# Reading the bias band backwards, warming TensorE with dummy matmuls, reordering and merging weight loads, and moving three copies to ScalarE in an attention kernel with T5 bias and a following feed-forward layer

## The chip, the cores and the metric

One core of one Trainium2 chip. The metric is the device time of one execution in microseconds (us), from the median of several executions. The granted TensorE clock of an execution is the mean over its span (1.00 is full speed). Ratios are computed as the mean time of one kernel's fast runs over that of the other kernel's fast runs of the same rounds on the same chip, with a 95% interval; so a ratio is not quite the ratio of the medians that stand beside it.

Engines: PE is TensorE, DVE is VectorE, ACT is ScalarE, POOL is GpSimd, SP is SyncE.

## The reference

Attention with a T5 relative-position bias over B=8, H=8, S=576, D=64, then a feed-forward layer over 4608 tokens (512 to 2048 to 512). Cut to what matters:

```python
scores = scale * np.matmul(q, k.transpose(0, 1, 3, 2))
bucket = ...                      # from |i - j|; constant for |i - j| >= 128
bias = bias_table[bucket]
scores = scores + bias.transpose(2, 0, 1)[None, :, :, :]
attn = softmax(scores)            # cut
attn_out = np.matmul(attn, v)
x = attn_out.transpose(0, 2, 1, 3).reshape(B * S, H * D)
h = x @ w_in
g = np.maximum(0.01 * h, h)
out = g @ w_out
```

The bias depends on the distance alone, and it is one constant from distance 128 on. So the kernel multiplies exp(score) by exp(bias minus that constant) inside a band around the diagonal and by nothing outside.

## The kernel before

The kernel works on 32 *pairs* (two heads of one batch; four pairs per batch) in program order. For a pair: copy q and k into rows (`pr`, DVE), transpose them (PE) and copy the result out of PSUM (`qt`, `kt`), score matmuls (`ps_s`, PE), exponential (`at`, `at4`, ACT), multiply by the band (DVE), then in the next pair's turn multiply by v (`ps_o`, called AV here, PE), normalise (`opair`, DVE) and transpose into `xT`. From pair 4 on, pieces of the feed-forward layer are put between these on PE.

The band: a row `ub` of 512 numbers per head is made from the bias table, written to DRAM (`u_row`) and read back as `hk`, in which each partition holds the row shifted by one. In `hk` the columns run the wrong way, so POOL (pairs 1 to 3) and DVE (pair 0) copy it reversed into `eb`, and a piece of that into `eb4` for the last 64 keys.

```python
nc.sync.dma_start(out=udr.ap(), in_=ub)                      # u_row
for h0, h1 in ((0, 2), (2, H)):
    nc.sync.dma_start(out=hk[:, h0:h1, :], in_=...)          # shifted by one per partition

def make_band(eng, p):
    t = hk[:, 2 * p : 2 * p + 2, :]
    eng.tensor_copy(out=eb[:, 2 * p : 2 * p + 2, :],
                    in_=...)                                 # t with its last step -1
    for e in range(2):
        r = slice(e * SL, (e + 1) * SL)
        eng.tensor_copy(out=eb4[r, p, :], in_=eb[r, 2 * p + e, e * SL : e * SL + P + SL])

load_qk(0, 2, H)
for i in range(NBUF):
    ...                                   # DVE clears v4, vn, kt, at, at4 of both buffers
load_v(0, 0, 2, True)
load_v(0, 2, H, False)
for j in range(1, n_pairs):
    make_band(nc.gpsimd, j)               # POOL waits here for hk
# ... cut ...
for n in range(N + 1):
    if n == 0:
        load_qk(1, 0, H)                  # all of these are issued by POOL, in this order
        load_w_in(0)                      # 4 loads of 256 KB
        load_w_in(1)                      # 4 loads
        load_v(1, 0, H, False)            # v of batch 1: needed by the AV of pair 4
        load_w_out()                      # 4 loads
    # ... cut ...

def band(n, u):
    # ... cut ...
    elif u == NJ + 1:
        o, m = at4[:, 3 * P : S], eb4[:, p, :]
    nc.vector.tensor_tensor(out=o, in0=o, in1=m, op=ALU.mult)
```

The softmax here doesn't subtract the row's maximum and nothing guards it: scores larger than these inputs give would overflow.

## Time and profile before

Median 418.32 us (three runs, 418.28 to 418.84). The profile is of one more execution, of 419.69 us (its span, first to last instruction, is 417.9 us).

| stretch of the profile before | PE busy |
|---|---|
| 0 to 60 us | 42.5 of 60 |
| 60 to 100 us | 38.2 of 40 |
| 100 to 200 us | 100.0 of 100 |
| 200 to 300 us | 100.0 of 100 |

After 60 us PE has next to no gaps, so time can only come from the first 60. The way to read those is by the start of each pair (its first 64x512 score matmul, from the timeline): 10.0, 15.1, 24.4, 30.6, 37.2, 45.2, 57.0 us, then every 8.5. The successor's start minus its own is a pair's length: pair 1 takes 9.3 and pair 5 takes 11.8 us, where neighbours take 6.3 and 8.5.

Busy time in windows of the kernel before. The columns are the window; its length; then PE, PE's weight loads, DVE, ACT and POOL, each as busy us and (instructions); the granted clock; the DMA share; GB/s:

```profile
20.00:25.00 5.00, 4.20 (x52) 2.94 (x50) 4.47 (x12) 2.92 (x4) 4.67 (x9) 1.00 0.01 3
...
45.00:50.00 5.00, 2.84 (x35) 1.48 (x35) 1.61 (x4) 3.02 (x4) 2.19 (x4) 1.00 1.72 183
50.00:55.00 5.00, 5.00 (x62) 2.98 (x58) 2.57 (x7) 2.69 (x4) 4.06 (x6) 0.66 1.24 207
```

At 20 to 25 the DMA engines move 3 GB/s: nothing is asked of them. At 45 to 50 PE has only 2.84 us of work, and then the clock falls to 0.66, so the 5.00 busy us that follow are partly slow ones.

Why nothing is asked of DMA is seen in POOL's timeline (start, us, engine, line, operation, out<-in, count, and in brackets what ended the idle time before it):

```profile
18.11 1.07 POOL L177 COPY eb<-hk 128x768 bf16<-128x768 bf16 x1 [3.79 <-DMA hk<-u_row]
...
23.98 0.81 POOL L109 DMA_DIRECT2D qn_100<-in_q_dram  x1
24.78 0.77 POOL L109 DMA_DIRECT2D kn_102<-in_k_dram  x1
25.54 3.24 POOL L204 DMA_DIRECT2D w_in_sb<-in_moe_w_in_dram  x6
...
35.08 0.89 POOL L125 DMA_DIRECT2D vn_104<-in_v_dram  x1 [1.37 <-DVE opair L327]
37.44 2.88 POOL L125 DMA_DIRECT2D vn_104<-in_v_dram  x3 [1.47 <-DMA w_in_sb<-in_moe_w_in_dram]
```

POOL waits 3.79 us for `hk`, copies until 24, and only then asks for the next batch and the weights. `vn_104` is v of batch 1; it stands behind both halves of `w_in`, and its last parts are asked for at 37.4 and later. The waits of PE in the first 62 us (what waits <- what it waits for: us, times, longest) and PE's timeline show where that ends:

```profile
PE ps_tq L231 <- DVE pr L223: 7.8, 1, 7.8
...
PE ps_o L321 <- DMA vn_104<-in_v_dram: 2.2, 2, 1.4
```

```profile
48.24 0.19 PE L321 MATMUL ps_o<-vn_104,at_109 128*128 128x65 bf16 x1 [1.41 <-DMA vn_104<-in_v_dram]
49.17 0.19 PE L321 MATMUL ps_o<-vn_104,at_109 128*128 128x65 bf16 x1 [0.74 <-DMA vn_104<-in_v_dram]
...
51.45 0.63 PE L347 MATMUL pm_865<-xT_92,w_in_sb 128*128 128x512 bf16 x1
...
55.15 0.38 PE L347 MATMUL pm_925<-xT_92,w_in_sb 128*128 128x512 bf16 x1
```

AV of pair 4 waits 2.2 us for v, and the same matmul that takes 0.38 us at 55 takes 0.63 at 51. Before pair 2 the chain of waits runs through the band: the row's write to DRAM, then `hk` for all heads:

```profile
4.99 4.93 DMA u_row<-ub
...
10.38 7.68 DMA hk<-u_row
...
18.11 1.08 POOL eb L177
```

Last, the band multiplies by form (mean ns in the middle, after the busy us):

```profile
L308 DVE TENSOR_TENSOR at_109<-at_109,eb 128x768 bf16<-128x768 bf16 x32 | 17.6, 552 | 16.3 <-ACT at_109 L279 16.3
...
L308 DVE TENSOR_TENSOR at_109<-at_109,eb 128x512 bf16<-128x512 bf16 x16 | 6.8, 424 | 20.5 <-ACT at_109 L279 20.3
```

### The profile page before, as it was taken

How to read it: one execution, taken by the hardware profiler on the slowest of the kernel's cores; microseconds unless marked ns; L12 is line 12 of the kernel's file. 1: busy time of each engine (PE TensorE's matmuls, PEld its weight loads, DVE VectorE, ACT ScalarE, POOL GpSimd, SP SyncE). 2: the span in 40 equal slices, each digit the busy share in tenths (PEclk: the TensorE clock that was granted, in tenths of full speed). 3: DMA queues.
4: the chain of work that ended last, by engine and by line, in shares of the span. 5: the costliest groups of instructions: out<-in, count | busy, mean ns of one | idle time of the engine just before them, and what ended most of it. 6: DMA issues, size and time to landing. Idle time of an engine off the chain costs nothing.

```text
span 417.9 us, 9069 instructions
## 1 busy us (share of the span) xinstructions
PE 394.9 (94%) x3872; PEld 203.8 (49%) x3872; DVE 226.7 (54%) x585; ACT 247.0 (59%) x339; POOL 67.9 (16%) x97
## 2 busy tenths in 40 slices
PE   1897699999999999999999999999999999999996
PEld 1365365455555555445554455555555454444442
DVE  6789667765666655655566666655666431010111
ACT  1768477866666676666666666667666633333310
POOL 8474631301022100410041004000000000000000
PEclk9999999999999999999999999999999999999999
DMA  8969999458027710944091706300000001010112
GB/s 115 131 99 202 183 204 166 36 33 140 27 37 71 123 44 27 83 75 91 25 83 30 137 27 39 46 25 27 27 27 27 27 27 50 25 52 25 52 50 76
DMA packets 60096, 29.16 MB, mean 70 GB/s; under 512 B 39056, under 2 KB 54424, under 8 KB 60056
## 3 DMA queue, kind: packets, MB, share of 16 engines
q0 software_dynamic: 53536, 18.36, 40.5%
q1 hardware_dynamic: 6520, 10.24, 6.8%
q8 instruction: 30, 0.49, 0.5%
q14 instruction: 10, 0.08, 0.1%
HBM read 37.49 MB, written 9.45 MB: 112 GB/s over the span
## 4 chain that ended last, share of the span: by engine, by line
PE 82%; DMA 8%; ACT 3%; POOL 2%; DVE 2%; issue 1%; SPq 0%
PE ps_o L321 7%; PE ps_s L259 6%; DMA w_in_sb<-in_moe_w_in_dram 3%; DMA vn_104<-in_v_dram 2%; PE ps_s L268 2%; PE ps_o L323 2%; DMA hk<-u_row 2%; PE ps_tx L335 2%; PE ps_tq L231 1%; PE ps_tk L242 1%; PE ps_s L265 1%; ACT at_109 L279 1%; DMA u_row<-ub 1%; PE pm_5795 L358 1%; PE pm_4291 L358 1%; PE pm_4115 L358 1%
## 5 line engine op out<-in xcount | busy, mean ns | idle before, releaser
L347 PEld LDWEIGHTS <-w_in_sb 128*128 128x128 bf16 x576 | 50.0, 98 | 73.3 <-issue 22.6
L279 ACT ACTIVATE at_109<-ps_s 128x1024 bf16<-128x1024 f32 x64 | 64.4, 1021 | 22.7 <-PE ps_s L259 22.6
L358 PEld LDWEIGHTS <-gt 128*128 128x128 bf16 x576 | 52.5, 98 | 51.4 <-issue 0.4
L279 ACT ACTIVATE at_110<-ps_s 128x1024 bf16<-128x1024 f32 x64 | 64.8, 1021 | 20.1 <-PE ps_s L259 20.1
L308 DVE TENSOR_TENSOR at_110<-at_110,eb 128x512 bf16<-128x512 bf16 (+1 forms) x64 | 32.5, 510 | 44.4 <-ACT at_110 L279 39.7
L308 DVE TENSOR_TENSOR at_109<-at_109,eb 128x512 bf16<-128x512 bf16 (+1 forms) x64 | 32.0, 505 | 39.0 <-ACT at_109 L279 36.6
L321 PEld LDWEIGHTS <-at_109 128*128 128x128 bf16 x640 | 29.3, 101 | 13.2 <-DVE opair L327 3.9
L327 DVE TENSOR_TENSOR opair<-ps_o,rcp 128x320 bf16<-128x320 f32 x64 | 31.5, 491 | 2.2
L321 PEld LDWEIGHTS <-at_110 128*128 128x128 bf16 x640 | 27.8, 99 | 10.0 <-DVE opair L327 3.0
L125 POOL DMA_DIRECT2D vn_104<-in_v_dram x16 | 14.2, 898 | 70.0 <-PE ps_o L323 39.9
L234 DVE COPY qt<-ps_tq 128x576 bf16<-128x576 bf16 x32 | 23.9, 747 | 0.5 <-PE ps_tq L231 0.5
L259 PE MATMUL ps_s<-qt,kt_107 64*128 64x512 bf16 x128 | 21.4, 403 | 2.1 <-DVE kt_107 L245 1.2
L125 POOL DMA_DIRECT2D vn_103<-in_v_dram x16 | 13.9, 881 | 55.5 <-PE ps_o L323 53.0
L231 PE MATMUL ps_tq<-ident,pr 96*128 96x96 bf16 x192 | 14.2, 213 | 7.9 <-DVE pr L223 7.8
L259 PE MATMUL ps_s<-qt,kt_108 64*128 64x512 bf16 x128 | 20.9, 398 | 0.7 <-ACT at_110 L279 0.3
L326 DVE RECIPROCAL rcp<-ps_o 128x5 f32<-128x5 f32 x64 | 12.2, 190 | 14.6 <-PE ps_o L323 14.6
L321 PE MATMUL ps_o<-vn_103,at_109 128*128 128x65 bf16 x320 | 16.1, 200 | 2.4 <-DVE opair L327 2.1
L321 PE MATMUL ps_o<-vn_104,at_109 128*128 128x65 bf16 x320 | 15.4, 197 | 2.2 <-DMA vn_104<-in_v_dram 2.2
L323 PEld LDWEIGHTS <-at_0_111 128*128 128x128 bf16 x160 | 16.1, 100 | 1.1 <-issue 0.8
L321 PE MATMUL ps_o<-vn_103,at_110 128*128 128x65 bf16 x320 | 15.1, 197 | 1.5 <-DVE opair L327 1.5
L281 ACT ACTIVATE at_110<-ps_s 128x512 bf16<-128x512 f32 x16 | 9.6, 598 | 10.9 <-PE ps_s L265 10.9
L323 PEld LDWEIGHTS <-at_1_112 128*128 128x128 bf16 x160 | 15.8, 98 | 0.2 <-DVE at_1_112 L308 0.2
(873 smaller groups left out, 814.7 us busy)
## 6 DMA issues: line engine op xcount, KB each, us to landing
out_dram<-y SPq DMA_DIRECT2D x36, 256.0 KB, 2.0
qn_100<-in_q_dram POOLq DMA_DIRECT2D x4, 576.0 KB, 6.1
kn_102<-in_k_dram POOLq DMA_DIRECT2D x4, 576.0 KB, 8.2
w_in_sb<-in_moe_w_in_dram POOLq DMA_DIRECT2D x8, 256.0 KB, 11.6
vn_104<-in_v_dram POOLq DMA_DIRECT2D x16, 128.0 KB, 4.9
w_out_sb<-in_moe_w_out_dram POOLq DMA_DIRECT2D x4, 512.0 KB, 10.0
qn_99<-in_q_dram POOLq DMA_DIRECT2D x3, 576.0 KB, 6.1
kn_101<-in_k_dram POOLq DMA_DIRECT2D x3, 576.0 KB, 9.4
```

What stands on the lines that cost most here:

```text
L125: nc.gpsimd.dma_start(out=vn[i][:, c, h0:h1, 0:D], in_=v[b, h0:h1, c * P : (c + 1) * P, :].rearrange("h s d -> s h d"),)
L231: nc.tensor.transpose(ps[:, c * RQ : (c + 1) * RQ], in_=qs[0:RQ, c, :], identity=ident[0:RQ, 0:RQ])
L234: nc.vector.tensor_copy(out=qt.rearrange("p (r c) -> p r c", c=NC), in_=ps[:, 0:S].rearrange("p (c r) -> p r c", c=NC))
L259: nc.tensor.matmul(ps[:, e, :], lhsT=kt[r, u * P : (u + 1) * P], rhs=qt[r, 0:512], start=True, stop=True)
L279: nc.scalar.activation(at[:, :, u, 0:512], ps, AF.Exp, scale=scale)
L308: nc.vector.tensor_tensor(out=o, in0=o, in1=m, op=ALU.mult)
L321: nc.tensor.matmul(ps[:, ic, :], lhsT=at[:, o : o + P], rhs=vn[i][:, c, 2 * p + e, :], start=(c == 0), stop=False)
L323: nc.tensor.matmul(ps[:, ic, :], lhsT=at4[:, ic * P : (ic + 1) * P], rhs=v4[i][:, p, e, :], start=False, stop=True)
L326: nc.vector.reciprocal(rcp, ps[:, :, D : D + 1])
L327: nc.vector.tensor_tensor(out=opair[:, :, e * D : (e + 1) * D], in0=ps[:, :, 0:D], in1=rcp.to_broadcast([P, NJ + 1, D]), op=ALU.mult)
L347: nc.tensor.matmul(pm, lhsT=w_in_sb[:, c, f * P : (f + 1) * P], rhs=xT[c][:, t0 : t0 + TT], start=(c == 0), stop=(c == n_cc - 1))
L358: nc.tensor.matmul(pm, lhsT=gt[:, f, ts * P : (ts + 1) * P], rhs=w_out_sb[:, f, :], start=(f == 0), stop=(f == n_fc - 1))
```

## The change

Its intent: take the reversing copies away by letting the multiplies read `hk` with a step of -1; fill PE's idle start so that its clock is released early; ask for the weights in fewer, larger loads, sooner, and for v of batch 1 between the two halves of `w_in`; and let ACT copy `qt` out of PSUM for pairs 1 to 3. The piece `eb4` becomes `hk4`, filled by two loads of its own. The clearing of the second buffers goes from DVE to POOL. The core of the diff, cut:

```diff
+    def clear(eng, i):
+        eng.memset(v4[i], 0.0)
+        ...                                  # v4's and vn's columns of ones
+        eng.memset(kts_[i][:, S : S + P], 0.0)
+        ...                                  # tails of at, at4
+    junk = per.tile([P, 512], BF16, name="junk")
+    nc.vector.memset(junk, 0.0)
+    clear(nc.vector, 0)
     ...
-    def make_band(eng, p):
-        ...
+    for e in range(2):
+        nc.sync.dma_start(
+            out=hk4[e * SL : (e + 1) * SL, :, :],
+            in_=bass.AP(tensor=udr, offset=e * UW + SL + P, ap=[[1, SL], [2 * UW, n_pairs], [1, P + SL]]),
         )
+    def mirrored(t, lo, hi):
+        ...                                  # columns lo:hi of the mirror image, step -1
     load_qk(0, 2, H)
-    for i in range(NBUF):
-        ...                                  # DVE's memsets
     load_v(0, 0, 2, True)
     load_v(0, 2, H, False)
-    for j in range(1, n_pairs):
-        make_band(nc.gpsimd, j)
+    clear(nc.gpsimd, 1)
+    load_qk(1, 0, H)

     def load_w_in(half):
-        for c in range(n_cc):
-            nc.gpsimd.dma_start(out=w_in_sb[:, c, o], in_=moe_w_in[c * P : (c + 1) * P, o])
+        nc.gpsimd.dma_start(out=w_in_sb[:, :, o], in_=moe_w_in[:, o].rearrange("(c p) f -> p c f", p=P))
     ...                                      # load_w_out: two loads instead of four
-        nc.vector.tensor_copy(out=qt..., in_=ps...)
+        if 0 < n < n_pairs:
+            nc.scalar.copy(out=o, in_=x)
+        else:
+            nc.vector.tensor_copy(out=o, in_=x)
     ...
         elif u == NJ + 1:
-            o, m = at4[:, 3 * P : S], eb4[:, p, :]
+            o, m = at4[:, 3 * P : S], mirrored(hk4[:, p, :], 0, P + SL)
     ...                                      # likewise the other multiplies, from hk
+    for _ in range(14):
+        nc.tensor.matmul(pw, lhsT=junk[:, 0:P], rhs=junk, start=True, stop=True)
     ...
             if n == 0:
-                load_qk(1, 0, H)
                 load_w_in(0)
+                load_v(1, 0, H, False)
                 load_w_in(1)
-                load_v(1, 0, H, False)
-                load_w_out()
+                load_w_out(0)
+                load_w_out(1)
```

## The prediction

> **What bounds it now.** PE. By stretches of the profile PE is busy 100.0 of 100 us at 100-200 and 200-300, and nearly all from 60 us to the tail; DVE (61%) and ACT (67%) have room there. Time can only come from the first 60 us, where PE is busy 42.5. By the timeline the score matmuls of each head pair start: pair 0 at 10.0, 1 at 15.1, 2 at 24.4, 3 at 30.7, 4 at 37.2, 5 at 45.2, 6 at 57.0, then every 8.5 us. Losses:
>
> - Pair 1 takes 9.3 us against 6.4 for its successors. Its band multiply waits for POOL's reversed copy (0.7 us), which waited for `hk` (POOL: 3.8 us, landed 18.05); and matmuls are slow: four 64x512 take 1.03 us before 26 us, 0.60 after.
> - Pairs 2 and 3: 6.3-6.5 us, DVE 89-92% busy.
> - Pair 5 takes 11.8 us, 3.4 too many: AV waits 2.2 us for `vn_104` (landed 49.1), PE then runs slow for 4 us (granted clock 0.66 at 50-55, matmuls 0.63 us, not 0.38). The chain of waits: `hk`, POOL copies to 24.0, qn/kn issue, `w_in` 11.0 us, `vn_104` 9.7 us. DMA moves 3 GB/s at 20-25, then about 200.
>
> **The change.**
> - The POOL copies (18.1-24.0) go. POOL instead clears second buffers (estimate 1.8 us, from 0.24 us for a 128x128 memset), so batch 1's q/k issue at about 16, not 24.0, w_in half 0 at 17.5, v behind it. Bytes over the 200 GB/s seen put v of batch 1 at 27-31, the second w_in half at about 36, before pairs 4-5 need them. I expect pair 5's 3.4 us back whole: the largest item.
> - DVE loses pair 0's copy, 0.36 + 0.42 us; the multiplies read backwards. The Trainium skill, "VectorE: DVE Perf Modes", "What auto-detection actually checks", allows step -1 in the paired 16-bit mode; the trace agrees for a copy (reversed 768 columns 0.36 us, forward 0.35). So multiplies stay 0.43 us (512) and 0.56 (768).
> - q copies of pairs 1-3 (0.75 us) go to ACT, estimate 0.65 from its 0.60 per 512 columns. DVE 6.5 to 5.75 per pair, ACT 5.3 to 6.0: saves 0.2-0.3 us per pair.
> - 14 dummy matmuls fill PE's idle 7.8 us. The Trainium skill, "TensorE: Matmul & The Clock Gate", "What's actually happening": about 3.4 us of sustained work releases the clock; the trace shows slow matmuls until 26 us. Estimate: dummies end near 7, pair 0 starts near 8.9, pair 1 near 13.9 (its k lands at 12.0).
> - Counterweight: two `hk4` loads behind `hk`; pair 0's last multiply now needs them. If they land near 18.5 in a busier DMA, AV 0 waits: pair 2 at 22.5-24 instead of 24.4.
>
> Sum: 0.5-2 us by pair 2, 0.5 in pairs 2-3, 3.4 in pair 5: about 5 us by pair 6. The rest, PE-bound, shifts unchanged.
>
> **Predicted: 413.3 us, 8 in 10 within 410.5 to 416.0.** Faster by over 2%: 0.12; within 2%: 0.86; slower: 0.02.
>
> **Right if:** pair 6 starts at 51-53, pair 5 takes 8.5; no AV wait on `vn_104`, no clock dip at 50-55; multiplies 0.43/0.56; first transposes already 0.43 us per six; no 3 GB/s slice; 100-300 still 100% PE.
>
> **Wrong if:** backward multiplies take one column per cycle [...]; dummies run past 8 us or don't release the clock; `hk4` lands after 20; early weight loads delay `hk` or batch 0's v; or another wait (xT, gt) surfaces in pair 5's place.

## The result, and the profile after

The changed kernel takes 416.76 us (median of 4, 415.84 to 417.02) against 418.30 for the kernel before on the same rounds (median of 4, 417.5 to 418.84): ratio 0.9961, 95% interval 0.9938 to 0.9984. So it is faster by some 1.5 us and within 2%, as thought most likely; but 413.3 was forecast, and 416.76 lies outside the range of 410.5 to 416.0.

The profile after is of an execution of 416.51 us. Pair starts in the profiles of both kernels (this table also holds the experiments told below; each row is one profiled execution, starts in us from the timeline):

| kernel | pair 0 | 1 | 2 | 4 | 5 | 6 | pair 5's length | time of that execution | clock |
|---|---|---|---|---|---|---|---|---|---|
| before | 10.0 | 15.1 | 24.4 | 37.2 | 45.2 | 57.0 | 11.8 | 419.69 | 0.996 |
| b_again | 10.0 | 15.1 | 23.9 | 37.2 | 45.1 | 57.5 | 12.4 | 420.19 | 0.992 |
| b_look1 | 10.0 | 15.1 | 24.3 | 37.8 | 45.7 | 55.7 | 10.1 | 418.40 | 0.996 |
| b_loads | 10.0 | 15.1 | 23.8 | 37.2 | 45.1 | 53.5 | 8.5 | 416.15 | 1.000 |
| b_loads_2 | 10.0 | 15.1 | 23.9 | 37.8 | 45.7 | 54.2 | 8.5 | 416.78 | 0.995 |
| b_order | 10.0 | 15.1 | 24.3 | 36.9 | 44.5 | 53.0 | 8.5 | 416.38 | 0.999 |
| after | 9.0 | 14.4 | 24.8 | 37.0 | 44.9 | 53.4 | 8.5 | 416.51 | 0.982 |
| a_again | 8.9 | 14.3 | 25.0 | 37.3 | 45.2 | 53.7 | 8.5 | 416.88 | 0.984 |
| a_third | 7.6 | 13.5 | 24.7 | 36.8 | 44.8 | 53.3 | 8.5 | 416.42 | 0.983 |
| a_nodummy | 7.5 | 14.0 | 25.1 | 37.4 | 45.4 | 53.9 | 8.5 | 416.89 | 1.000 |
| a_qdve | 8.3 | 13.7 | 25.2 | 37.5 | 45.5 | 54.0 | 8.5 | 417.09 | 0.983 |
| a_direct | 8.8 | 14.5 | 24.3 | 36.5 | 44.5 | 53.0 | 8.5 | 416.12 | 0.982 |
| a_direct_kt | 7.9 | 14.8 | 23.3 | 35.4 | 43.4 | 51.9 | 8.5 | 414.92 | 0.988 |
| a_direct_kt_2 | 9.1 | 14.5 | 23.3 | 35.8 | 43.8 | 52.3 | 8.5 | 415.46 | 0.983 |
| a_late_hk | 9.1 | 14.5 | 23.8 | 36.1 | 44.3 | 52.8 | 8.5 | 415.45 | 0.983 |
| a_late_hk_2 | 8.1 | 14.2 | 23.2 | 35.4 | 43.6 | 52.1 | 8.5 | 414.69 | 0.986 |
| a_fill | 8.0 | 15.9 | 23.7 | 35.9 | 43.9 | 52.3 | 8.5 | 415.44 | 0.992 |
| a_noband | 8.1 | 13.5 | 21.8 | 34.1 | 42.1 | 50.6 | 8.5 | 413.73 | 0.987 |

Take the start of pair 6 from the time of the execution: 419.69 - 57.0 = 362.7 before, 416.51 - 53.4 = 363.1 after, 413.73 - 50.6 = 363.1 for the fastest, and between 362.6 and 363.4 in every row. What follows pair 6 is the same in all of them, to 0.8 us. The whole study is thus about when pair 6 starts, and a median time gives that start too: 418.3 - 362.7 = 55.6 for a typical execution of the kernel before. The profiled one, with 57.0, was 1.4 us later than that.

The windows after:

```profile
10.00:15.00 5.00, 3.60 (x27) 1.48 (x25) 1.14 (x3) 4.76 (x7) 3.36 (x11) 0.53 1.85 186
15.00:20.00 5.00, 2.45 (x26) 1.49 (x26) 2.64 (x9) 1.94 (x3) 4.15 (x7) 0.50 1.46 221
20.00:25.00 5.00, 4.93 (x64) 3.27 (x62) 3.79 (x11) 3.33 (x5) 3.01 (x4) 0.60 1.28 208
...
45.00:50.00 5.00, 4.74 (x70) 2.66 (x69) 2.98 (x8) 4.43 (x6) 0.88 (x2) 1.00 1.27 207
50.00:55.00 5.00, 4.69 (x53) 2.53 (x50) 3.77 (x11) 4.13 (x7) 1.25 (x2) 1.00 1.67 192
```

The second half is what was hoped for: PE has 4.74 us of work at 45 to 50, the clock stays at 1.00 at 50 to 55, and the 3 GB/s of 20 to 25 have become 208. The first half is new: the clock is at half speed from 10.3 to 24, and at 15 to 20 PE has 2.45 us of work (before: 4.55). POOL's timeline shows the loads:

```profile
15.05 0.81 POOL L109 DMA_DIRECT2D qn_100<-in_q_dram  x1
...
17.37 1.78 POOL L125 DMA_DIRECT2D vn_104<-in_v_dram  x2
20.11 1.76 POOL L125 DMA_DIRECT2D vn_104<-in_v_dram  x2 [0.96 <-DMA vn_103<-in_v_dram]
```

v of batch 1 is asked for by 22 us, not 40, and no AV waits for it any more. But two new waits stand before pair 2. First the waits of PE, then those of DVE:

```profile
PE ps_o L329 <- DVE at_0_111 L314: 2.2, 2, 2.1
```

```profile
DVE at_0_111 L314 <- DMA hk_98<-u_row: 2.3, 1, 2.3
...
DVE kt_108 L256 <- POOL kt_108 L140: 1.6, 1, 1.6
```

Their place is seen in DVE's timeline:

```profile
14.98 0.37 DVE L256 COPY kt_108<-kt_108 64x64 bf16<-64x64 bf16 x2 [1.57 <-POOL kt_108 L140]
15.38 1.77 DVE L314 TENSOR_TENSOR at_109<-at_109,hk 128x512 bf16<-128x512 bf16 x4
19.46 0.26 DVE L314 TENSOR_TENSOR at_0_111<-at_0_111,hk_98 128x192 bf16<-128x192 bf16 x1 [2.32 <-DMA hk_98<-u_row]
```

(`hk_98` is `hk4`; `at_0_111` is `at4` of even pairs.) DVE stands still for 1.57 us because POOL has not yet cleared the tail of the second `kt`: the memset that the change moved from DVE to POOL stands behind POOL's loads of v. Then the four multiplies of pair 0 run (1.77 us), and the fifth, the small one, waits 2.32 us for `hk4`. The chain of waits of that stretch shows how late `hk4` is:

```profile
4.97 4.50 DMA u_row<-ub
...
11.16 8.18 DMA hk_98<-u_row
...
19.46 0.27 DVE at_0_111 L314
```

The row's write begins at 4.97 us, as before (4.99). The start of PE's timeline has the dummies:

```profile
1.23 5.99 PE L414 MATMUL ps_w<-junk 128*128 128x512 bf16 x14 [1.23 <-DVE junk L145]
7.05 0.42 PE L235 MATMUL ps_tq<-ident,pr 96*128 96x96 bf16 x6
```

And the backward multiplies by form:

```profile
L314 DVE TENSOR_TENSOR at_109<-at_109,hk 128x768 bf16<-128x768 bf16 x32 | 17.6, 553 | 16.2 <-ACT at_109 L286 16.1
...
L314 DVE TENSOR_TENSOR at_109<-at_109,hk 128x512 bf16<-128x512 bf16 x16 | 6.8, 424 | 20.4 <-ACT at_109 L286 20.3
```

424 ns forward and 424 backward; 552 forward and 553 backward.

### The profile page after: what moved, and what is told of

Same layout as the page of the kernel before. It is cut to its first block, busy times and chain, and to the rows that moved or that the text cites. A ratio compares the mean times of both kernels' runs of the same rounds, so it can differ in the third digit from the quotient of the medians.

```text
span 414.7 us, 9081 instructions
## 1 busy us (share of the span) xinstructions
PE 397.0 (96%) x3886; PEld 204.0 (49%) x3886; DVE 222.7 (54%) x573; ACT 248.2 (60%) x342; POOL 59.8 (14%) x87
## 4 chain that ended last, share of the span: by engine, by line
PE 83%; DVE 7%; ACT 4%; DMA 3%; issue 1%; SPq 0%; DVEq 0%; ACTq 0%
PE ps_o L327 8%; PE ps_s L266 7%; PE ps_s L275 2%; DMA hk_98<-u_row 2%; PE ps_o L329 2%; PE ps_tx L341 2%; PE ps_tq L235 1%; ACT at_109 L286 1%; ACT at_110 L286 1%; PE ps_tk L249 1%; DVE at_109 L314 1%; PE ps_s L272 1%; DMA u_row<-ub 1%; DVE opair L333 1%; ACT gt L355 1%
## 5 line engine op out<-in xcount | busy, mean ns | idle before, releaser
L314 DVE TENSOR_TENSOR at_110<-at_110,hk 128x512 bf16<-128x512 bf16 (+1 forms) x64 | 32.2, 506 | 44.5 <-ACT at_110 L286 40.6
L314 DVE TENSOR_TENSOR at_109<-at_109,hk 128x512 bf16<-128x512 bf16 (+1 forms) x64 | 32.0, 506 | 38.6 <-ACT at_109 L286 36.4
L327 PEld LDWEIGHTS <-at_109 128*128 128x128 bf16 x640 | 28.5, 99 | 10.3 <-DVE opair L333 3.0
L327 PEld LDWEIGHTS <-at_110 128*128 128x128 bf16 x640 | 27.2, 98 | 9.6 <-DVE opair L333 3.0
L242 DVE COPY qt<-ps_tq 128x576 bf16<-128x576 bf16 x29 | 21.7, 748 | 1.8 <-PE ps_tq L235 1.8
L332 DVE RECIPROCAL rcp<-ps_o 128x5 f32<-128x5 f32 x64 | 12.2, 191 | 11.6 <-PE ps_o L329 11.6
L327 PE MATMUL ps_o<-vn_103,at_109 128*128 128x65 bf16 x320 | 16.3, 200 | 1.1 <-DVE opair L333 0.7
L329 PEld LDWEIGHTS <-at_0_111 128*128 128x128 bf16 x160 | 15.9, 99 | 2.5 <-DVE at_0_111 L314 2.5
L327 PE MATMUL ps_o<-vn_103,at_110 128*128 128x65 bf16 x320 | 14.5, 194 | 1.7 <-DVE opair L333 1.7
L329 PE MATMUL ps_o<-v_0_105,at_0_111 128*128 128x65 bf16 x80 | 13.8, 200 | 2.2 <-DVE at_0_111 L314 2.2
L329 PEld LDWEIGHTS <-at_1_112 128*128 128x128 bf16 x160 | 15.6, 97 | 0.2 <-DVE at_1_112 L314 0.2
L341 PEld LDWEIGHTS <-opair 128*128 128x128 bf16 x160 | 11.3, 98 | 7.6 <-DVE opair L333 0.9
## 6 DMA issues: line engine op xcount, KB each, us to landing
w_in_sb<-in_moe_w_in_dram POOLq DMA_DIRECT2D x2, 1024.0 KB, 13.5
```

Source lines behind the costliest of these rows:

```text
L242: nc.vector.tensor_copy(out=o, in_=x)
L327: nc.tensor.matmul(ps[:, ic, :], lhsT=at[:, o : o + P], rhs=vn[i][:, c, 2 * p + e, :], start=(c == 0), stop=False)
L329: nc.tensor.matmul(ps[:, ic, :], lhsT=at4[:, ic * P : (ic + 1) * P], rhs=v4[i][:, p, e, :], start=False, stop=True)
L332: nc.vector.reciprocal(rcp, ps[:, :, D : D + 1])
L341: nc.tensor.transpose(ps[:, ic * P : (ic + 1) * P], in_=opair[:, ic, :], identity=ident)
```

## The experiments

Two things had to be explained: why pair 2 starts at 24.8 instead of the forecast 22.5 to 24, and why the 3.4 us of pair 5, which did vanish from the profile, are not in the time. Sixteen runs were made in four groups, each group on one chip with its own runs of the kernel before (medians 418.90, 418.49, 419.58 and 418.72 us, 11 runs each; the shared runs hold for every kernel of a group). Unless told otherwise a kernel gave the right result, was timed with 6 runs, and all runs were fast. The theories are named in the expectations themselves; a letter there holds for that run.

### The kernel before, once more: b_again (first group) and b_look1 (third group)

No edit.

> The kernel before, unchanged, against itself. The profile of before came from an execution timed at 419.69 us while the median of the others is 418.3, so it may hold a loss that most executions don't have. Theory A (part of pair 5's 3.4 us in that profile was chance): the new profile shows pair 6 starting about 1.4 us earlier than 57.0 (55 to 56), and no dip of the granted clock to 0.5 at 51-54, or a dip elsewhere; the spans of the five rounds spread over 1 us with the mean clock. Rival B (the profile is typical): pair 6 again at 57.0 within 0.3 and the same dip. Either way the ratio is 1.000 within 0.002.

> The kernel before, one more profile. Profiled executions of it took 419.69 and 420.19 us with pair 6 at 57.0 and 57.5; others between 417.4 and 419.8. Theory A (pair 5's loss varies from execution to execution with where the clock falls): time and start of pair 6 move together, time minus start near 362.7; a time of 418 goes with pair 6 at 55.3 or so. Rival B (a profile always shows 57 and its time is always above 419.5): again 57.0 to 57.6.

b_again: 419.51 us against 418.90, ratio 1.0014 (0.9992 to 1.0037). b_look1: a single run of 418.40 us, state unknown. The profiled execution of b_again was a still slower one (420.19 us), with pair 6 at 57.5 rather than where a typical one was expected, so this look missed a typical execution. That of b_look1 was a quicker one, and its pair 6 starts at 55.7. Its windows:

```profile
35.00:40.00 5.00, 5.00 (x81) 3.43 (x78) 4.70 (x13) 2.87 (x5) 3.35 (x4) 0.66 1.12 206
...
50.00:55.00 5.00, 4.60 (x65) 2.86 (x64) 4.15 (x11) 3.35 (x5) 3.96 (x6) 1.00 1.24 207
```

Here the clock fell at 35 to 40 and not at 50 to 55; AV still waits for v (1.5 us), and pair 5 takes 10.1 us, not 11.8. So the wait for v is in all three profiles of this kernel, and the slow stretch inside pair 5 is in two of them (b_again has one at 35 to 40 as well).

The 51 executions of this kernel whose mean clock was recorded agree. In 18 the mean clock was 0.998 or more: median 417.98 us, 417.37 to 418.90. In the other 33 it was 0.992 to 0.996: median 419.56 us, 418.05 to 420.40. A lower mean clock goes with 1.6 us at the medians (the ranges overlap), and whether it comes changes from run to run of one program; where the clock fell is known for the three profiled executions alone. The profiled 419.69 was thus of the commoner kind: the 418.3 from which the forecast subtracts is the median of three executions, and the medians of the four groups' own 11 are 418.49 to 419.58.

### The loads alone, added to the kernel before: b_loads (first group) and b_loads_2 (fourth)

```diff
-        for c in range(n_cc):
-            nc.gpsimd.dma_start(out=w_in_sb[:, c, o], in_=moe_w_in[c * P : (c + 1) * P, o])
+        nc.gpsimd.dma_start(out=w_in_sb[:, :, o], in_=moe_w_in[:, o].rearrange("(c p) f -> p c f", p=P))
 ...                                     (load_w_out: two loads)
                 load_w_in(0)
-                load_w_in(1)
                 load_v(1, 0, H, False)
-                load_w_out()
+                load_w_in(1)
+                load_w_out(0)
+                load_w_out(1)
```

POOL's copies stay, so the loads are still asked for at 24 us.

> The kernel before with only the weight loads changed: two w_in halves and two w_out halves of one descriptor batch each, v of batch 1 issued between the w_in halves. POOL still copies the bands until 24.0. Theory A (pair 5's loss was the late v of batch 1, and the order alone cures it): v lands before 42 us instead of 49.1, the AV of pair 4 doesn't wait, pair 5 takes 8.5 us, pair 6 starts near 53.7, time 1.5 to 3.4 us below before, thus as fast as the changed kernel or faster. Rival B (the earlier issue at 15 us was needed): v lands after 45, pair 5 takes over 10 us, gain under 1 us.

> The kernel before with only the weight loads merged and v of batch 1 in between. Theory A (the order of the loads is the whole of what the change gained, and the band, dummies, clears and ACT copies add up to nothing): within 0.7 us of the changed kernel of the same rounds. Rival B (the other parts cost something): 0.7 us or more below the changed kernel. Rival C (they gain something): 0.7 us or more above it.

b_loads: 416.11 us, ratio 0.9942 (0.9921 to 0.9963). b_loads_2: 416.95 us, ratio 0.9955 (0.9934 to 0.9977), beside a_third (the changed kernel, same chip) with 416.73 and 0.9954. The loads alone give what the whole change gives. Asking for them 9 us earlier is not needed.

### One line of order: b_order (third group)

```diff
                 load_w_in(0)
-                load_w_in(1)
                 load_v(1, 0, H, False)
+                load_w_in(1)
                 load_w_out()
```

> The kernel before with one line moved: v of batch 1 is loaded between the two halves of w_in instead of after both; the loads stay as small as before. Theory A (the order alone cures pair 5): v lands before 44 us, pair 5 takes 8.5 to 8.8 us, ratio as with merged loads, 0.993 to 0.996. Rival B (merging is needed[...]): v lands at 42 to 47, AV of pair 4 waits 0.5 us or more, ratio 0.996 to 0.999.

416.27 us, ratio 0.9932 (0.9911 to 0.9952). No AV waits for v; a wait for `w_in` takes its place, but a small one, as PE's waits show:

```profile
PE pm L347 <- DMA w_in_sb<-in_moe_w_in_dram: 0.8, 1, 0.8
```

Pair 7 takes 9.2 us for 8.5 there. Merging the loads isn't needed either: the order of v and the second half of `w_in` is the gain. On this chip, where the kernel before has a median of 419.58, the medians are 3.3 us apart, so what pair 5's wait costs depends on how many executions have the lower clock.

### The changed kernel, once more: a_again (second group) and a_third (fourth)

No edit.

> The changed kernel unchanged, for the same chip and rounds as the three below, and a second profile of it. Pair 2 starts within 0.4 us of 24.8, pair 6 within 0.4 us of 53.4, ratio to before 0.994 to 0.997. If its profile again shows a wait of DVE for hk4 of about 2.3 us and slow matmuls from about 10.7 to 24 us, the first profile was typical.

> The changed kernel once more, to stand beside the three below on one chip. Ratio 0.995 to 0.9965; time of the profiled execution minus start of pair 6 is 362.7 to 363.4, as in every profile so far.

a_again: 416.55 us, ratio 0.9950 (0.9930 to 0.9970). a_third: 416.73 us, 0.9954 (0.9931 to 0.9978). Pair 2 starts at 25.0 and 24.7, so 24.8 was no accident, and it doesn't follow pair 0, which starts at 8.9 in one and 7.6 in the other. DVE's wait for `hk4` is 1.2 and 1.8 us there, less than the 2.3 expected, and its wait for POOL's memset is 1.8 in both.

### Without the dummies: a_nodummy (first group)

```diff
-    for _ in range(14):
+    for _ in range(0):
         nc.tensor.matmul(pw, lhsT=junk[:, 0:P], rhs=junk, start=True, stop=True)
```

> The changed kernel without the 14 dummy matmuls. In the changed kernel's profile the clock was released for 7.0 to 10.7 us only and then fell until 24. Theory A (the dummies buy almost nothing because PE is too idle between 8 and 20 us to hold the clock, and pair 1's k lands at 11.4 anyway): pair 0 starts near 8.4 instead of 9.0 (the transposes start at 5.2 instead of 7.05, at the slow rate), pair 1 within 0.4 of 14.4, pair 2 within 0.5 of 24.8, time within 0.6 us of the changed kernel. Rival B (the dummies are worth something): pair 2 over 0.8 us later and time over 0.8 us longer.

416.96 us, ratio 0.9957 (0.9937 to 0.9978): as good as with them. Without dummies pair 0 starts at 7.5 us, no later than with them: by DVE's timelines, what brought pair 0 forward from 10.0 is that DVE no longer clears both sets of buffers (5.01 to 7.4 us) just before its first `pr` copy: it clears the first set at 1.2 to 2.4, before the bias table's work, and POOL clears the second. That copy is at 4.87 us, and at 7.35 in the kernel before.

### The q copies back on DVE: a_qdve (third group)

```diff
-        if 0 < n < n_pairs:
+        if False:
             nc.scalar.copy(out=o, in_=x)
```

> The changed kernel with the q copies of pairs 1 to 3 back on DVE. In the profiles with ACT copying, pairs 2 and 3 take 6.1 us each; the kernel before takes 6.1 to 6.3 and 6.5 to 7.3. Theory A (the move to ACT is worth 0.3 to 0.7 us per pair in pairs 2 and 3, nothing in pair 1, which waits for the band): pair 2 starts within 0.4 of 24.8, pairs 2 and 3 together take 12.7 to 13.6 us instead of 12.2, time 0.5 to 1.2 us longer than the changed kernel (ratio 0.995 to 0.9961), so 0.997 to 0.9985. Rival B (worth nothing, or a loss because ACT's copy delays pair 0's exponentials): time within 0.3 us of the changed kernel or less.

416.97 us, ratio 0.9949 (0.9930 to 0.9969). From pair 2's start to pair 4's it takes 37.53 - 25.16 = 12.4 us; the changed kernel takes 12.1 to 12.3 in its three profiles. ACT's copies are worth 0.2 us at most, which these runs don't resolve.

### Pair 0 without hk4: a_direct (first group)

```diff
         elif u == NJ + 1:
+            if n == 0:
+                for e in range(2):
+                    r = slice(e * SL, (e + 1) * SL)
+                    oo = at4[r, 3 * P : S]
+                    nc.vector.tensor_tensor(out=oo, in0=oo,
+                                            in1=mirrored(hk[r, e, :], e * SL, e * SL + P + SL), op=ALU.mult)
+                return
             o, m = at4[:, 3 * P : S], mirrored(hk4[:, p, :], 0, P + SL)
```

For pair 0 the needed columns are already in `hk`, which lands first; two small multiplies take the place of one.

> The changed kernel, but pair 0's last multiply reads the band from hk in two halves of 64 partitions instead of hk4, so nothing waits for hk4 at pair 0. Theory A (the hk4 wait of 2.3 us ate the gain before pair 2): AV 0 runs through at 17-18 us, pair 2 starts at 22.3 to 23.3 instead of 24.8, pair 6 1.5 to 2.5 us earlier than 53.4, time 1.5 to 2.3 us below the changed kernel's 416.8, so about 414.7. Rival B (the slow matmuls after the clock fell at 10.7 us set pair 1's length): pair 2 still at 24.3 or later, gain under 0.5 us. Rival C: the multiplies of pair 1 then wait for hk's second load (landing near 18), pair 2 at 23.5 to 24, gain about 1.

415.92 us, ratio 0.9932 (0.9911 to 0.9953), with the wait for `hk4` gone. But pair 2 starts at 24.3, only 0.5 us sooner, for a wait of 2.3. DVE's timeline has the reason:

```profile
16.04 0.37 DVE L256 COPY kt<-kt 64x64 bf16<-64x64 bf16 x2 [1.75 <-POOL kt L140]
16.43 1.76 DVE L321 TENSOR_TENSOR at<-at,hk 128x512 bf16<-128x512 bf16 x4
18.11 0.51 DVE L315 TENSOR_TENSOR at<-at,hk 64x192 bf16<-64x192 bf16 x2
```

The wait for POOL's memset, which `hk4` had hidden, is now what ends last. In this execution the memset came 1 us later than in the profile after; in a_again, where it came as late (DVE goes on at 15.84), the wait for `hk4` was 1.2 us and pair 2 started at 25.0.

### Both waits away: a_direct_kt (second group) and a_direct_kt_2 (fourth)

```diff
-        eng.memset(kts_[i][:, S : S + P], 0.0)
 ...
     nc.vector.memset(junk, 0.0)
+    for t in kts_:
+        nc.vector.memset(t[:, S : S + P], 0.0)
     clear(nc.vector, 0)
```

added to a_direct: DVE clears both `kt` tails at its start, as the kernel before did.

> Two of the new waits taken away from the changed kernel: pair 0's last multiply reads hk directly, not hk4, and the clear of the second kt buffer stands on DVE at the start instead of behind the v loads on POOL. Theory A (in the first of these alone, the POOL clear took over: DVE waited 1.75 us for it and the multiplies began at 16.4 instead of 15.4): the multiplies of pair 0 start at 15.2 to 15.5 (then hk's own landing binds), pair 2 starts at 23.0 to 23.6 instead of 24.3, pair 6 at about 52.0, time 0.7 to 1.3 us below the version with the first alone (415.9 on its chip, ratio 0.9932), so a ratio near 0.990 to 0.9915. Rival B (slow matmuls bind): pair 2 at 24.0 or later.

> The changed kernel with the two new waits (hk4, POOL's clear of the second kt buffer) taken away. Theory A (those two waits are what swallowed the gain of the other parts): 1.2 to 2.2 us below the changed kernel of the same rounds, and 1 us or more below the version with the load order alone. Rival B (the difference seen before came from another chip): under 0.7 us below.

a_direct_kt: 414.94 us, ratio 0.9911 (0.9892 to 0.9931), with a_again at 416.55 on the same chip. a_direct_kt_2: 414.70 us, 0.9907 (0.9887 to 0.9927), with a_third at 416.73. So 1.6 and 2.0 us less than the changed kernel, twice; pair 2 starts at 23.3 in both. In the second the clock reads 0.50 all through 12 to 24 us, as in the changed kernel, so slow matmuls alone (rival B) do not hold pair 2 at 24.0 or later. The memset alone, with `hk4` kept, was not tried. In a_direct_kt DVE is done with the copies of pair 1's k (`kt`) at 15.04, and its first multiplies then wait only for `hk` itself, 0.55 us (in a_direct_kt_2 `hk` landed at 15.19 and they began at 15.30):

```profile
12.70 0.36 DVE L228 COPY pr<-kn 96x768 bf16<-96x768 bf16 x1 [2.73 <-DMA kn<-in_k_dram]
...
14.61 0.43 DVE L257 COPY kt<-kt 64x64 bf16<-64x64 bf16 x2
15.58 1.77 DVE L322 TENSOR_TENSOR at<-at,hk 128x512 bf16<-128x512 bf16 x4 [0.55 <-DMA hk<-u_row]
```

This version beats both kernels.

### No band to wait for: a_noband (second group; wrong result)

a_direct_kt, in which pairs 0 and 1 multiply by a tile of ones that ACT makes at the start:

```diff
+    ones = per.tile([P, 2, 3 * P], BF16, name="ones")
+    for e in range(2):
+        nc.scalar.activation(ones[:, e, :], junk[:, 0 : 3 * P], AF.Exp)
 ...
-        hp = hk[:, 2 * p : 2 * p + 2, :]
+        hp = ones if n < 2 else hk[:, 2 * p : 2 * p + 2, :]
```

and likewise in the last multiply. It asks what the start would give if the band were there in time.

> WRONG RESULT on purpose: as the version with both waits taken away, but the multiplies of pairs 0 and 1 read a tile of ones that ACT makes at the start, so they wait for no band at all; the loads stay. Theory A (the band's chain, u_row written in 4.5 us, then hk in 5.3 us, landing near 15.2, is what the head start of pair 0 runs into): pair 0's multiplies start near 14.0 to 14.6, pair 2 at 22.0 to 22.8. Rival B (ACT's exponentials, ending at 15.1, and PE at the slow rate bind by then): pair 2 within 0.4 us of the version with both waits taken away, so the hk landing costs nothing.

413.77 us, ratio 0.9888 (0.9865 to 0.9910); its relative error is 0.024, as meant. The first multiplies run 2 us sooner than in a_direct_kt, and pair 2 starts at 21.8:

```profile
12.15 0.76 DVE L256 COPY kt<-ps_tk 128x576 bf16<-128x576 bf16 x1 [0.52 <-PE ps_tk L253]
12.95 0.66 DVE L260 COPY kt<-kt 64x64 bf16<-64x64 bf16 x2
13.64 1.76 DVE L325 TENSOR_TENSOR at<-at,ones 128x512 bf16<-128x512 bf16 x4
```

Not all of these 2 us are the band's. Pair 1's k was copied from 11.28 us on in this execution and from 12.70 in a_direct_kt (11.3 to 12.7 in the profiles of the changed kernel's variants), so DVE was done with `kt` 1.4 us sooner; the band itself held DVE for the 0.55 us shown above. The medians are 1.2 us apart, and the intervals of the ratios overlap. That 413.77 is close to the forecast 413.3 is luck: the forecast had its gain elsewhere.

### More dummies: a_fill (second group)

a_direct_kt with further dummy matmuls between the stages of pairs 0 and 1, to keep the clock up:

```diff
+    def fill(k, t):
+        for _ in range(k):
+            nc.tensor.matmul(t, lhsT=junk[:, 0:P], rhs=junk, start=True, stop=True)
 ...
+    fill(5, pw)                      # and 2, 2, 2, 4, 4 further on
```

> As the version with both waits taken away, with 21 more dummy matmuls at places in pairs 0 and 1 where PE waits for ACT or DVE, so that the clock stays released from 7 us on. Theory A (the fall of the clock at 10.7 to 24 us costs pair 1 about 1 us, because AV, transposes and scores between 16 and 24 stand in its chain: five groups of AV 1.4 us slow, 0.75 fast, transposes 0.67 and 0.43): granted clock 1.00 at 10-25, pair 2 0.8 to 1.5 us earlier than in that version, time lower by as much. Rival B (the fillers take the time that they give back, or the clock falls anyway): pair 2 within 0.3 us or later.

414.85 us, ratio 0.9910 (0.9887 to 0.9934), where a_direct_kt had 414.94: no gain at the medians. In the profiled execution (415.44 us, mean clock 0.992) the clock fell all the same, and was back at 18.6 us, for 21.8 in a_direct_kt:

```profile
6.00:11.00 5.00, 3.54 (x35) 1.50 (x32) 2.19 (x5) 2.56 (x3) 3.88 (x6) 1.00 1.40 183
11.00:12.00 1.00, 0.29 (x4) 0.00 (x0) 0.00 (x0) 0.88 (x1) 0.00 (x0) 0.88 2.31 150
12.00:17.00 5.00, 4.15 (x24) 1.45 (x26) 3.23 (x9) 2.80 (x5) 4.37 (x11) 0.50 1.52 234
```

This execution, in which the dummies also put pair 1 off to 15.9, is no test of what a released clock is worth in pairs 0 and 1, since the clock wasn't kept. But one profile is one execution here too. The other five were two with mean clocks of 0.992 and 0.994 (416.49 and 415.34 us) and three with 0.998 to 1.000, which took 413.97, 414.24 and 414.36 us: each less than the quickest of a_direct_kt (414.37), whose six have 0.981 to 0.988. That the clock was kept in these three, and is worth some 0.7 us (414.24 against 414.94), is likely; they were not profiled, so it isn't shown.

### Fewer bytes beside hk: a_late_hk (third group) and a_late_hk_2 (fourth)

a_direct_kt, with SP loading `hk` for heads 0 to 3 only, and POOL loading the rest of `hk` and `hk4` later, behind v of batch 0:

```diff
-    for h0, h1 in ((0, 2), (2, H)):
-        nc.sync.dma_start(out=hk[:, h0:h1, :], ...)
-    for e in range(2):
-        nc.sync.dma_start(out=hk4[e * SL : (e + 1) * SL, :, :], ...)
+    load_hk(nc.sync, 0, 2)
+    load_hk(nc.sync, 2, 4)
 ...
     load_v(0, 2, H, False)
+    load_hk(nc.gpsimd, 4, H)
+    for e in range(2):
+        load_hk4(nc.gpsimd, e)
```

> A try for a better version: the changed kernel with both new waits taken away, and the parts of hk and hk4 that pairs 2 and 3 need loaded later, from POOL behind v of batch 0, so that they don't share the DMA with hk of pair 0 and k of pairs 1 to 3. Theory A (what is left of the wait is hk landing at 15.3 to 15.6 in a full DMA): hk of pair 0 lands by 14.5, pair 0's multiplies start by 14.7, pair 2 at 22.2 to 23.0, time 0.4 to 1.1 us below the version with both waits taken away (ratio 0.9911), thus 0.9885 to 0.990. Rival B (hk's landing is its fixed latency, not shared bandwidth): hk at 15.2 or later, no gain.

> The same with hk and hk4 of pairs 2 and 3 loaded later from POOL. Its first profile showed hk of pair 0 landing at 15.7, no earlier, so I expect no gain: within 0.5 us of the version with the two waits taken away. If it is 0.5 us or more below, shared bandwidth does matter.

a_late_hk: 414.35 us, ratio 0.9880 (0.9858 to 0.9901). a_late_hk_2: 414.59 us, 0.9898 (0.9878 to 0.9918), with a_direct_kt_2 at 414.70 and 0.9907 on the same chip. The first multiplies of pair 0 begin at 15.77 us after waiting 1.24 us for `hk`, and at 15.58 in a_direct_kt: the load that pair 0 needs lands no sooner. Whether this is better than a_direct_kt by a tenth of a us can't be told; it isn't worse.

## Why the prediction was wrong

**What bounds the kernel** was right. PE is at 100.0 of 100 us in both stretches after too, and the rest after pair 6 shifts unchanged (362.6 to 363.4 us in every profile).

**Pair 5 coming back whole** was right in kind and wrong in size. "I expect pair 5's 3.4 us back whole": pair 5 takes 8.5 us in all profiles with v ahead of the second half of `w_in`, and b_order shows that the order alone does it. But 3.4 us is the loss of the profiled execution of 419.69 us, in which the clock fell inside pair 5. I took it off 418.3, the median. By an estimate from the table, an execution of 418.3 has pair 6 at 418.3 - 362.7 = 55.6 and a pair 5 of 55.6 - 45.2 = 10.4 us, so only 1.9 us were to be had there, and 1.6 in the execution of b_look1 (10.1 to 8.5). The term was too large by about 1.5 us. The mistake is one of bookkeeping: a term read from an execution has to be taken from the time of that execution.

**"0.5-2 us by pair 2"** was the step that failed. Pair 2 starts later, not sooner: 24.8 (24.7 to 25.0 in three profiles) against 24.4 (23.9 to 24.4). That is 0.7 us lost on the means, 24.83 less 24.16, where 1.2 in the middle were to be won: off by 1.9 us. Pair 0 came forward as forecast (8.9 forecast, 9.0 in the profile), pair 1 nearly so (13.9 and 14.4). But in the changed kernel the time of pair 2 isn't set by them; what ends last before it comes of the band, whose chain starts at 4.97 us (4.99 in the kernel before) and wasn't sped up. The change took POOL's and DVE's copies out of that chain and put two other things in:

- `hk4` as a load of its own. The forecast had this as a counterweight that would end at 22.5 to 24, for a landing near 18.5, and called it dangerous only after 20. It landed at 19.3 (11.16 + 8.18), and that was enough for 24.8.
- the clear of the second `kt` on POOL. The forecast costed it as 1.8 us of POOL's time that nothing would wait for. DVE waited for it 1.57 us. Since the wait for `hk4` hides the other, undoing `hk4`'s alone gave little (a_direct: pair 2 at 24.3), and undoing both gave 1.5 us (a_direct_kt: 23.3), and 1.6 to 2.0 us of time.

**Pairs 2 and 3** were forecast to win 0.5. From pair 2's start to pair 4's it is 12.8 us in the profile before and 12.2 after, so the size is right, but the reason given isn't shown: with the copies back on DVE (a_qdve) it is 12.4. In the other profiles with POOL's copies it is 12.6 to 13.9. What makes pair 3 quicker without the change's copies on ACT was not taken apart.

**The dummies** did what was said of the clock at first, and it was worth nothing. The Trainium skill, "TensorE: Matmul & The Clock Gate", "What's actually happening", says that some 3.4 us of sustained work release the clock and that its window is free-running, so that the moment varies. The traces agree that it varies: the 14 dummies took 5.99 us in one execution, 4.93 and 4.65 in two others. In the first that is 0.43 us each, all slow, so the release took nearly 6 us of work there. The first six transposes then took 0.42 us, for 0.66 without dummies (a_nodummy). But the clock fell again at about 10.3 us (0.67 in 10 to 11 us, 0.50 after), before the matmuls that mattered, and DVE, the band and the loads set the pace anyway (a_nodummy: the same time).

**The backward multiplies** were right. The Trainium skill, "VectorE: DVE Perf Modes", "What auto-detection actually checks", lets a step of -1 take part in the paired 16-bit mode; the trace agrees, with 424 ns for both directions at 512 columns and 553 for 552 at 768.

**The sum.** Start from the profiled 419.69. Take off 3.3 for pair 5 (11.8 less 8.5) and 0.6 for pairs 2 and 3, add 0.4 for pair 2 (24.8 less 24.4), and 416.2 is left, for 416.51 measured in the profile after; the rest is 0.4 in the tail behind pair 6 (363.1 for 362.7) less rounding. By these estimates the forecast's error, 416.76 - 413.3 = 3.5, is made of 1.9 at pair 2 and some 1.5 at pair 5, and the small rest is in the noise.

**What stays open.** What decides where the clock falls in the kernel before. That the wait for v brings the fall inside pair 5 on is likely, since it follows a stretch in which PE has 2.84 us of work in 5, but b_look1 has the wait without the fall, and b_loads_2 has a fall at 35 to 40 without the wait. How much of the 1.2 us between a_direct_kt and a_noband (414.94 and 413.77) a quicker way to make the band would give. Whether a clock kept up through pairs 0 and 1 is what made three executions of a_fill some 0.7 us quicker.

## What to carry to other kernels

A profile is one execution: before you subtract a loss that you read in it, compare its time with the median, and ask whether the loss is there in every execution. When you take work out of a chain, follow every input of the step at its end; a memset moved to an idle engine stands behind that engine's queue of loads (1.57 us of waiting here), and a new small load can land last of all (19.3 us here). And try the one-line part first: moving one load ahead of another gave what the whole rewrite gave, and the rewrite had 1.6 to 2.0 us more to give once the two waits that it had added were gone.

## What the Trainium skill lacked or had wrong

- "Vector Engine (DVE) Microarchitecture Reference", "5.1 Performance modes — why throughput varies by op and dtype", lists how an operand with a negative step streams as not measured. Here a two-source multiply of 16-bit operands with a second input of step -1 took 424, 492 and 553 ns at 512, 640 and 768 columns, and 424, 491 and 552 with step +1.
- "TensorE: Matmul & The Clock Gate", "What's actually happening", has the slow state come back after an idle window of about 3.4 us, and no share of busy time at which a window counts as idle. Here the clock fell at 10.34 us, with PE busy 1.82 of the 3.40 us before, and in a_fill at 11.76 us, with PE busy 1.65 of 3.40 (the times follow from the clock of the slices, 0.67 at 10 to 11 and 0.88 at 11 to 12, taken as 1.00 before the fall and 0.50 after).
- No page says that the granted clock of a profile can read 1.00 at the head of a kernel where matmuls still run slow. In the kernel before it reads 1.00 at 10 to 25 us, where four 64x512 matmuls take 1.03 us; they take 0.60 to 0.61 when the clock is released.
- "DMA: Bandwidth & Descriptors", "Anatomy of one DMA — SWDGE (gpsimd) path", gives about 2 us as the fixed cost of a load that POOL issues, and that section says nothing of SP's. Here an 8 KB write on SP's queue, with POOL's loads under way, took 4.50 us in the profile after and 5.20 in a_again, and a 96 KB read behind three others on that queue 8.18. The page's section "Queues, rings and completion order" says that a completion lands after every earlier write of the same DMA engine, across queues, which would fit; no run here takes it apart, and no page gives the delay.
